# Attention and a two-layer expert on one core: short products ahead of expert pieces, 1/l ahead of the maxima, x's split spread out, and three engines' order left to the list

## Chip, cores and metric

The kernel runs on one core of a Trainium2 chip. The metric is device time in microseconds, of one launch. Lower is better.

## What is computed

For 4 batches and 8 heads of 576 positions by 64 features the reference computes causal softmax attention, mixes it with a linear memory read-out, and passes the result (2304 tokens by 512) through an expert of two matrices with a softplus between them:

```python
scores = scale * q @ k.T                      # causal mask: -1e9 above the diagonal
a = exp(scores - scores.max(-1)); a /= a.sum(-1) + 1e-09
local = a @ v
q_p = phi(q)                                  # elu(q) + 1
mem_out = (q_p @ M_prev) / (q_p @ z_prev + 1e-6)
x = g * mem_out + (1 - g) * local             # g = sigmoid(beta), one per head
h = x @ w_in                                  # 512 -> 2048
out = softplus(h) @ w_out                     # 2048 -> 512
```

## The kernel before

**Attention.** The work is cut into 16 units, one for each batch and pair of heads. A unit has four slots: the first holds query chunks 0 and 1 (128 rows each), then chunk 2, chunk 3, and the 64 rows of chunk 4. In a slot, `emit_S` puts the scores of both heads into one of two PSUM tiles `s` on TensorE (with small matmuls that add the mask), VectorE takes the row maxima (`nm`), ScalarE scales them and computes the exponentials `P` with their row sums `l`. One slot later `emit_split` forms r = 1/l on VectorE (`rr`), multiplies P by r on GpSimd into a half-precision high part, and subtracts that on VectorE into a low part (both in `PHL`). DMAs on SP's queue transpose PHL into `PTA` or `PTB`. Three slots after the chunks 0 and 1, and three after chunk 4, `emit_pv` multiplies with v into the PSUM tile `xp`, and ScalarE writes x out of it.

**Preparation of a unit.** `prep_items` spreads over the slots of the unit before: sums of |v| on ScalarE (`jk`, `sm`), a product with a matrix of means on TensorE (`sp`), five short instructions on VectorE (`sc`), phi(q) (`pe`, `ph`), v in two halves (`vb`), and the memory read-out: five products (`np`, function `f3`) whose denominators and quotient (`a`, `mem`) VectorE computes. The second part of `np` lies in the same PSUM tile as `xp`, of which there is one.

**Expert, first part.** Of the 16 blocks of 128 hidden units the first six (`GA`) are computed beside the attention for four blocks of 384 tokens. `fill_step` puts one piece into a slot: twelve matmuls for one h (`hp`), or eighteen for one output quarter (`op`). Each x block must be split first into two tiles of a reduced format (`xhl`, GpSimd casts, VectorE subtracts). `emit_g` applies softplus and splits the result into `g` on ScalarE and VectorE. The weights come as 64-bit floats; `split64` decodes them on GpSimd, VectorE and ScalarE, twelve half-blocks during the attention, let out at `WRATE` per slot.

**Expert, rest.** After the attention the remaining weights are decoded and the rest of the expert runs, with TensorE's, VectorE's, ScalarE's and GpSimd's instructions ordered by the compiler's list.

**What sets the order.** From the loads of the first unit to the end of the attention the loop in `attn_softplus_moe` writes the order by hand: TensorE, VectorE, ScalarE and GpSimd run their instructions in the order in which Python emits them (`tc.manual_schedule`), and each engine waits at the first one that isn't ready. SP's queue alone is ordered by the list: the compiler's own timing of the program decides, among the ready instructions of an engine, by the place at which they were emitted. In a slot the loop emits: the posts of the last piece (softplus and both halves of g), the scores and maxima, then `emit_split` of the slot before, the products with v that are due, the expert piece, and the preparation that is due.

Of the kernel before, what the change touches and what calls it, by code (L numbers as in the profile page):

```python
# [11 lines left out]
F32R = mybir.dt.float32r  # L12
# [17 lines left out]
GRPS = [6, 10]  # L30
NWB = 6
PVLAG = 3
WRATE = 0.6
GA = GRPS[0]


# [10 lines left out]
def attn_softplus_moe(  # L47
# [35 lines left out]
    CAP = 384  # L83
# [88 lines left out]
    def emit_g(pool, hp, n, cap, gb):  # L172
        l = pool.tile([128, cap], F32, tag="l", name="l", bufs=3)[:, :n]
        g = pool.tile([128, 2, cap], F32R, tag="g", name="g", bufs=gb)
        A.activation(out=l, in_=hp[:, :n], func=AF.Softplus)  # L175
        cast(A, g[:, 0, :n], l)
        sub(V, g[:, 1, :n], l, g[:, 0, :n])
        return g

    def out_pairs(f, g, dm, n):  # L180
        w = wt[f]
        wh, wl = w[:, 1, 0, dm * 128:(dm + 1) * 128], w[:, 1, 1, dm * 128:(dm + 1) * 128]
        return [(wh, g[:, 0, :n]), (wh, g[:, 1, :n]), (wl, g[:, 0, :n])]

    blocks, work, ready, posts = deque(), deque(), {}, deque()
    XLAG = 2

    def split_x(pool, t0, kd, xt, ea, eb):
        src = x[:, kd, t0:t0 + CAP]
# [3 lines left out]
    def push_fill(k):  # L193
        st = {}
        t0 = k * CAP

        def xs():
            st["x"] = moe1.tile([128, 2, 4, CAP], F32R, tag="xhl", name="xhl", bufs=1)
            for kd in range(4):
                split_x(moe1, t0, kd, st["x"], P, V)  # L200

        def h(f):
            hp = emit_h(moe1, f, st["x"], CAP, CAP)

            def post():
                st[f] = emit_g(moe1, hp, CAP, CAP, GA)
            return post

        def o(dm):
            op = ps_r.tile([128, 512], F32, tag="h", name="op", bufs=2)  # L210
            pairs = []
            for f in range(GA):
                pairs += out_pairs(f, st[f], dm, CAP)
            mm3(op[:, :CAP], pairs, True, True)

            def post():
                pb = moe1.tile([128, CAP], F32, tag="l", name="pb", bufs=3)
                A.copy(pb, op[:, :CAP])
                SY.dma_start(out=part[:, dm, t0:t0 + CAP], in_=pb)
            return post  # L220

        blocks.append((k, xs))
        work.extend([(12, k, h, f) for f in range(GA)] + [(3 * GA, k, o, dm) for dm in range(4)])

    def next_block(t):
        if blocks:
            k, xs = blocks.popleft()
            xs()
            done.add(k)
            ready[k] = t + XLAG  # L230

    def fill_step(t, force=False):

        if not work:
            return
        n, k, fn, j = work[0]
        if k not in done:
            next_block(t)  # L240
        if not force and ready.get(k, 1 << 30) > t:
            return
        work.popleft()
        posts.append(fn(j))
        if n == 12 and j == GA - 1:
            next_block(t)

    def run_posts():
        while posts:
            posts.popleft()()  # L250


    units = [Unit(b, p) for b in range(B) for p in range(NP)]
# [126 lines left out]
            w = 1  # L380
        return pts, l[:, :w]

    def emit_split(u, cs, pts, l):
        r = at.tile([128, 4], F32, tag="rr", name="rr", bufs=3)[:, :l.shape[1]]
        p = u.p
        if cs == (4,):
            ci = cinv4[:, p:p + 1]
        else:
            ci = cinv[:, 2 * p:2 * p + 2].unsqueeze(1).to_broadcast([128, len(cs), 2])
        V.scalar_tensor_tensor(out=r if cs == (4,) else r.rearrange("p (c h) -> p c h", h=2),  # L390
                               in0=l if cs == (4,) else l.rearrange("p (c h) -> p c h", h=2),
                               scalar=1e-9 * ESH, in1=ci, op0=ALU.add, op1=ALU.mult)
        V.reciprocal(out=r, in_=r)
        w = "A" if cs[0] < 2 else "B"
        if w not in u.pt:
            shape = [128, 8, 256] if w == "A" else [128, 18, 320]
            u.pt[w] = at.tile(shape, F16, tag="PT" + w, name="PT" + w, bufs=2 if w == "B" else 1)
        dst = u.pt[w]
        for j, c in enumerate(cs):
            pt = pts[j]  # L400
            ph = at.tile([128, (c + 1) * 512 if c < 4 else 2 * S], F16, tag=f"PHL{c}", name="PHL", bufs=1)
            if c < 4:
                nk = c + 1
                o = ph.rearrange("p (k t h s) -> p k t h s", t=2, h=2, s=128)
                for h in range(2):
                    rh = r[:, 2 * j + h:2 * j + h + 1]
                    src = pt[:, h * nk * 128:(h + 1) * nk * 128].rearrange("p (k s) -> p k s", s=128)
                    P.tensor_scalar(out=o[:, :, 0, h, :], in0=src, scalar1=rh, scalar2=0.0, op0=ALU.mult, op1=ALU.add)  # L408
                    V.scalar_tensor_tensor(out=o[:, :, 1, h, :], in0=src, scalar=rh, in1=o[:, :, 0, h, :],  # L409
                                           op0=ALU.mult, op1=ALU.subtract)  # L410
                q0 = (c - (0 if w == "A" else 2)) * 128
                SY.dma_start_transpose(out=dst[:, 0:4 * nk, q0:q0 + 128], in_=ph)
            else:
                o = ph[:, 0:1024].rearrange("p (k t s) -> p k t s", t=2, s=128)
                src = pt[:, 0:512].rearrange("p (k s) -> p k s", s=128)
                o4, s4 = ph[:, 1024:1152], pt[:, 512:576]
                P.tensor_scalar(out=o[:, :, 0, :], in0=src, scalar1=r, scalar2=0.0, op0=ALU.mult, op1=ALU.add)
                P.tensor_scalar(out=o4[:, 0:64], in0=s4, scalar1=r, scalar2=0.0, op0=ALU.mult, op1=ALU.add)
                V.scalar_tensor_tensor(out=o[:, :, 1, :], in0=src, scalar=r, in1=o[:, :, 0, :], op0=ALU.mult,
                                       op1=ALU.subtract)  # L420
                V.scalar_tensor_tensor(out=o4[:, 64:128], in0=s4, scalar=r, in1=o4[:, 0:64], op0=ALU.mult,
                                       op1=ALU.subtract)
                d = dst.rearrange("p (j h) q -> p j h q", h=2)
                for h in range(2):
                    SY.dma_start_transpose(out=d[:, :, h, 256:320], in_=ph[64 * h:64 * h + 64, 0:1152])
# [51 lines left out]
    with ExitStack():  # L477
# [3 lines left out]
        consts(bsb)  # L481
        order = ExitStack()
        order.enter_context(tc.manual_schedule(engines={
            mybir.EngineType.PE, mybir.EngineType.DVE, mybir.EngineType.Activation, mybir.EngineType.Pool}))
        loads(0)
        prep, late = {}, {}

# [18 lines left out]
        decode = deque()  # L506
        t = 0
        while t < ns or late or prev is not None:
            cur = None
            if t < ns:  # L510
                i, c = slots[t]
                u = units[i]
                if c[0] == 0 and i + 1 < len(units):
                    loads(i + 1)
                    plan(i + 1, t)
                run_posts()
                cur = (u, c) + emit_S(u, c)
                if c[0] in (0, 4):
                    late.setdefault(t + PVLAG, []).append((u, "A" if c[0] == 0 else "B"))
            else:  # L520
                run_posts()
            if prev is not None:
                emit_split(*prev)
            for a in late.pop(t, []):
                emit_pv(*a)
            fill_step(t)
            for f in prep.pop(t, []):
                f()
            if decode:
                a, b = decode.popleft()  # L530
                a()
                posts.append(b)
            wcred += WRATE
            while wcred >= 1 and pieces:
                wcred -= 1
                decode.append(pieces.popleft()())
            prev = cur
            t += 1
        run_posts()
        assert not pieces and not prep and not decode  # L540

        order.close()
        attn_ctx.close()
        while work and work[0][1] in done:
            fill_step(t, True)
            run_posts()
        wb = ctx.enter_context(tc.tile_pool(name="wb", bufs=1, side="right", reuse_waits="tile"))
        hcnt.append(0)
        moe2 = ctx.enter_context(tc.tile_pool(name="moe2", bufs=1, reuse_waits="tile"))
# [33 lines left out]
        for i in range(len(seq) + LAG):  # L583
            if i < len(seq):
                s, f = seq[i]
                fl = steps[s][2]
                fi = f - fl[0]
                hp = emit_h(moe2, f, xh[s], CAP, CAP)
                gs[i] = emit_g(moe1, hp, CAP, CAP, GA)
                for _ in range(2 if i % 3 == 0 else 1):  # L590
                    if pieces:
                        pieces.popleft()()
                if fi == 0:
                    if s == len(rest):
                        partial(s)
                    if s + 1 < len(steps):
                        partial(s + 1)
                if s + 1 < len(steps) and 1 <= fi < 5:
                    next_x(s + 1, fi - 1)
# [81 lines left out]
```

## Time and profile before

| what | value |
|---|---|
| median of 3 runs | 722.59 us (721.75 to 723.76) |
| profiled execution, its own time | 720.95 us |
| span from the first to the last instruction in the profile | 719.2 us |
| TensorE matmul busy | 599.6 us (83%) |
| VectorE busy | 413.5 us (57%) |
| ScalarE busy | 313.8 us (44%) |
| GpSimd busy | 125.9 us (18%) |
| mean granted TensorE clock | 0.898 |

The profile is one execution. PE is TensorE's matmuls, PEld its weight loads, DVE VectorE, ACT ScalarE, POOL GpSimd, SPq the DMA queue. L409 is line 409 of the kernel before. The shares are averages over two stages that differ: the attention with the expert's first part, to about 416 us, and the expert alone after it.

### The profile page before, as it was taken

The numbers are of one execution on the slowest core, as the hardware profiler recorded it, in microseconds if no ns is written. First come the engines' busy times: TensorE is split into PE (matmuls) and PEld (weight loads), VectorE is DVE, ScalarE is ACT, GpSimd is POOL, SyncE is SP. The second block draws the span as 40 slices with busy tenths as digits, with TensorE's granted clock in tenths as the row PEclk, the third lists the DMA queues.
The fourth block names the chain that finished last, engine by engine and source line by source line (L and its number), as shares of the span: only waits on it lengthen the run. The fifth ranks groups of instructions, "written<-read, shape, count | busy, mean of one in ns | idle before, by whom it ended". The sixth has DMA issues, their size and how long they took to land.

```text
span 719.2 us, 10758 instructions
## 1 busy us (share of the span) xinstructions
PE 599.6 (83%) x3928; PEld 527.3 (73%) x3928; DVE 413.5 (57%) x918; ACT 313.8 (44%) x797; POOL 125.9 (18%) x218
## 2 busy tenths in 40 slices
PE   6553553847986679989888999999999999999998
PEld 4332332636864557767666899999999999999997
DVE  4788787887578785777678368886203122220211
ACT  6444544357565564665466245444213232321221
POOL 1323223322124231223123112220000000000000
PEclk9566756769997898989999999999999999999999
DMA  5656556435576564644743455571200202010001
GB/s 186 140 123 163 149 111 164 118 72 130 119 160 129 104 128 96 152 91 100 150 85 68 101 173 192 205 226 67 73 16 23 67 0 88 1 45 1 22 23 45
DMA packets 125749, 73.87 MB, mean 103 GB/s; under 512 B 105728, under 2 KB 115456, under 8 KB 125696
## 3 DMA queue, kind: packets, MB, share of 16 engines
q1 hardware_dynamic: 125696, 73.18, 41.2%
q8 instruction: 31, 0.51, 0.3%
q14 instruction: 22, 0.18, 0.1%
HBM read 38.03 MB, written 9.44 MB: 66 GB/s over the span
## 4 chain that ended last, share of the span: by engine, by line
PE 64%; DVE 23%; ACT 5%; issue 3%; POOL 3%; DMA 1%; SPq 0%; ACTq 0%; POOLq 0%
PE hp L153 26%; PE acc L153 21%; DVE PHL L409 7%; PE op L153 7%; PE xp L443 5%; DVE nm L357 4%; DVE mem L318 2%; PE xp L433 2%; ACT P L364 2%; POOL PHL L408 2%; PE s L343 1%; DVE xhl L91 1%; PE s L370 1%; DVE wu L139 1%; DVE wu L141 1%
## 5 line engine op out<-in xcount | busy, mean ns | idle before, releaser
L153 PE MATMUL hp<-xhl,w 128*128 128x384 f32 x1152 | 220.8, 341 | 3.5 <-DVE a L315 3.5
L153 PEld LDWEIGHTS hp<-xhl,w 128*128 128x128 f32 x1152 | 202.4, 189 | 6.1 <-issue 3.7
L153 PE MATMUL acc<-g,w 128*128 128x384 f32 x864 | 161.6, 337 | 0.1
L153 PEld LDWEIGHTS acc<-g,w 128*128 128x128 f32 x864 | 151.7, 188 | 0.6 <-DVE pl L617 0.4
L91 DVE TENSOR_TENSOR g<-l,g 128x384 fp32r<-128x384 f32 x96 | 53.7, 560 | 139.9 <-ACT g L97 139.0
L175 ACT ACTIVATE l<-hp 128x384 f32<-128x384 f32 x96 | 46.9, 490 | 155.3 <-PE hp L153 153.1
L408 POOL TENSOR_SCALAR PHL<-P,rr 128x128 f16<-128x128 f32 (+3 forms) x128 | 67.9, 546 | 233.6 <-ACT nm L360 131.4
L409 DVE SCALAR_TENSOR_TENSOR PHL<-P,rr,PHL 128x128 f16<-128x128 f32 (+3 forms) x128 | 88.5, 739 | 35.4 <-POOL PHL L408 35.4
L343 PE MATMUL s<-kp,mq 64*128 64x128 f32 (+3 forms) x256 | 57.5, 536 | 27.2 <-ACT P L364 16.3
L433 PE MATMUL xp<-identf,mem 128*128 128x128 f32 (+1 forms) x80 | 21.2, 351 | 68.9 <-DVE mem L318 67.2
L433 PEld LDWEIGHTS xp<-identf,mem 128*128 128x128 f32 (+1 forms) x80 | 10.5, 167 | 80.5 <-issue 75.0
L364 ACT ACTIVATE P<-s,nm 128x128 f32<-128x128 f32 (+3 forms) x128 | 66.1, 525 | 4.1 <-ACT nm L360 0.4
L153 PE MATMUL op<-g,w 128*128 128x384 f32 x288 | 54.9, 344 | 1.0 <-DVE g L91 1.0
L357 DVE TENSOR_REDUCE nm<-s 128x2 f32<-128x256 f32 (+1 forms) x64 | 50.9, 816 | 3.7 <-PE s L352 3.7
L443 PEld LDWEIGHTS <-vb 128*64 128x64 f16 x640 | 41.5, 142 | 15.3 <-issue 3.0
L153 PEld LDWEIGHTS op<-g,w 128*128 128x128 f32 x288 | 50.0, 190 | 2.5 <-DVE g L91 1.3
L97 ACT CAST w<-wu 128x512 fp32r<-128x512 f32 x32 | 19.9, 621 | 73.3 <-DVE wu L141 73.3
L360 ACT ACTIVATE nm<-nm 128x2 f32<-128x2 f32 (+1 forms) x48 | 9.8, 204 | 96.3 <-DVE nm L357 96.3
L97 ACT CAST g<-l 128x384 fp32r<-128x384 f32 x96 | 49.2, 513 | 2.6
L343 PEld LDWEIGHTS s<-kp,mq 64*128 64x128 f32 x256 | 21.3, 203 | 37.1 <-ACT P L364 19.0
L443 PE MATMUL xp<-PTB,vb 128*64 128x320 f16 (+2 forms) x448 | 45.0, 378 | 0.0
L137 POOL TENSOR_SCALAR wu<-ws 128x512 f32<-128x512 f32 x32 | 29.3, 915 | 66.9 <-DMA ws<-in_w_in_dram 35.7
(74 smaller groups left out, 583.7 us busy)
## 6 DMA issues: line engine op xcount, KB each, us to landing
ws<-in_w_in_dram SPq DMA_DIRECT2D x16, 512.0 KB, 3.9
ws<-in_w_out_dram SPq DMA_DIRECT2D x16, 512.0 KB, 3.5
mq<-in_nat_dram SPq DMA_DIRECT2D x16, 353.0 KB, 3.4
pl<-part SPq DMA_DIRECT2D x7, 768.0 KB, 5.9
va<-in_nat_dram SPq DMA_DIRECT2D x16, 320.0 KB, 3.2
kp<-in_nat_dram SPq DMA_DIRECT2D x16, 288.0 KB, 3.7
out_dram<-pl SPq DMA_DIRECT2D x24, 192.0 KB, 1.9
part<-pb SPq DMA_DIRECT2D x16, 192.0 KB, 2.1
```

The costliest lines, as they stand in the source:

```text
L91: eng.tensor_tensor(out=out, in0=in0, in1=in1, op=ALU.subtract)
L97: A.copy(out, in_)
L137: P.tensor_scalar(out=tu, in0=sw[:, :, 1], scalar1=RB, scalar2=1.0, op0=ALU.mult, op1=ALU.mult)
L153: nc.tensor.matmul(out, lhsT=l, rhs=r, start=start and i == 0, stop=stop and i == n - 1)
L175: A.activation(out=l, in_=hp[:, :n], func=AF.Softplus)
L343: return mm(s[:, h, o:o + n], lhsT=u.qp[rows[h], c * 128:(c + 1) * 128], rhs=u.kp[rows[h], :n], start=True, stop=True, skip_group_check=True)
L357: V.tensor_reduce(out=nm[:, 2 * j:2 * j + 2], in_=s[:, :, o:o + n], op=ALU.max, axis=AX.X, negate=True)
L364: A.activation(out=pts[j][:, h * n:h * n + n], in_=s[:, h, o:o + n], func=AF.Softplus, scale=SCALE, bias=nm[:, 2 * j + h:2 * j + h + 1], a ...
L408: P.tensor_scalar(out=o[:, :, 0, h, :], in0=src, scalar1=rh, scalar2=0.0, op0=ALU.mult, op1=ALU.add)
L409: V.scalar_tensor_tensor(out=o[:, :, 1, h, :], in0=src, scalar=rh, in1=o[:, :, 0, h, :], op0=ALU.mult, op1=ALU.subtract)
L433: nc.tensor.matmul(xp[:, c * 128 - q0:min(c * 128 + 128, S) - q0], lhsT=u.mem[r, c, :], rhs=identf[r, r], start=c in (0, 2), stop=False, i ...
L443: nc.tensor.matmul(xp[r, lo:n], lhsT=u.vb[:, vi, kc, r], rhs=pt[:, kc * 4 + t * 2 + h, lo:n], start=False, stop=kc == kcs[-1] and i == len ...
```

## The change

Six edits. (1) The hand-written order is kept on TensorE alone; VectorE, ScalarE and GpSimd get the list's order too. (2) In a slot the preparation, with its short products `sp` and `np`, is emitted ahead of the expert piece. (3) The function that forms r is cut out of `emit_split` as `emit_r` and emitted ahead of the scores. (4) The low half of g is emitted after the products with v and not with the high half. (5) The four parts of an x block's split are emitted one or two to a slot, and a block that isn't fetched ahead is ready after three slots, not two. (6) `WRATE` goes from 0.6 to 0.5. What is computed stays the same, with as many instructions of each kind.

```diff
-WRATE = 0.6
+WRATE = 0.5
...
         cast(A, g[:, 0, :n], l)
-        sub(V, g[:, 1, :n], l, g[:, 0, :n])
-        return g
+        return g, lambda: sub(V, g[:, 1, :n], l, g[:, 0, :n])
...
-        def xs():
-            st["x"] = moe1.tile([128, 2, 4, CAP], F32R, tag="xhl", name="xhl", bufs=1)
-            for kd in range(4):
-                split_x(moe1, t0, kd, st["x"], P, V)
+        def xs(kd):
+            if kd == 0:
+                st["x"] = moe1.tile([128, 2, 4, CAP], F32R, tag="xhl", name="xhl", bufs=1)
+            split_x(moe1, t0, kd, st["x"], P, V)
...
             def post():
-                st[f] = emit_g(moe1, hp, CAP, CAP, GA)
+                st[f], lo = emit_g(moe1, hp, CAP, CAP, GA)
+                los.append(lo)
...
-    def next_block(t):
+    def next_block(t, step):
         if blocks:
             k, xs = blocks.popleft()
-            xs()
+            xq.extend([(t + 1 + kd // step, lambda kd=kd: xs(kd)) for kd in range(4)])
             done.add(k)
-            ready[k] = t + XLAG
+            ready[k] = t + 1 + 4 // step
...
-    def emit_split(u, cs, pts, l):
+    def emit_r(u, cs, pts, l):
         r = at.tile([128, 4], F32, tag="rr", name="rr", bufs=3)[:, :l.shape[1]]
...
         V.reciprocal(out=r, in_=r)
+        return r
+
+    def emit_split(u, cs, pts, r):
...
         order.enter_context(tc.manual_schedule(engines={
-            mybir.EngineType.PE, mybir.EngineType.DVE, mybir.EngineType.Activation, mybir.EngineType.Pool}))
+            mybir.EngineType.PE}))
...
-            cur = None
+            cur, rr = None, None
+            run(posts)
+            if prev is not None:
+                rr = emit_r(*prev)
...
             if prev is not None:
-                emit_split(*prev)
+                emit_split(*prev[:3], rr)
             for a in late.pop(t, []):
                 emit_pv(*a)
-            fill_step(t)
+            run(los)
             for f in prep.pop(t, []):
                 f()
+            fill_step(t)
+            split_due(t)
```

How instructions move is shown at three places. Numbers behind a name (`w_170`, `mask_66`) tell tiles of one kind apart. First TensorE, in a unit with expert pieces, around the memory read-out `np`. Before:

```order
L153 MATMUL hp<-xhl,w_171 128x384 x12
L314 MATMUL np<-mq,ph 128x130 x5
L343 MATMUL s<-kp,mq 128x512 x2
...
L433 MATMUL xp<-identf,mem 128x128 x2
L433 MATMUL xp<-identf,mem 128x64
...
L153 MATMUL op<-g,w_166 128x384 x3
...
L287 MATMUL sp<-sm,mean 128x1
```

With the change:

```order
L317 MATMUL np<-mq,ph 128x130 x5
L153 MATMUL hp<-xhl,w_170 128x384 x12
L346 MATMUL s<-kp,mq 128x512 x2
...
L439 MATMUL xp<-identf,mem 128x128 x2
L439 MATMUL xp<-identf,mem 128x64
...
L290 MATMUL sp<-sm,mean 128x1
...
L153 MATMUL hp<-xhl,w_171 128x384 x12
```

The expert piece of twelve now stands between `np` and the products into `xp`, and `sp` stands ahead of the next piece. Second VectorE, in the second slot of a unit, where chunk 2's maxima, the split of chunks 0 and 1 and the quotient `mem` meet. Before:

```order
L357 TENSOR_REDUCE nm<-s 128x2
L390 SCALAR_TENSOR_TENSOR rr<-l,cinv 128x4
L393 RECIPROCAL rr<-rr 128x4
L409 SCALAR_TENSOR_TENSOR PHL<-P,rr,PHL 128x128 x2
L409 SCALAR_TENSOR_TENSOR PHL<-P,rr,PHL 128x2x128 x2
L315 TENSOR_SCALAR a<-np 128x6
...
L318 TENSOR_TENSOR mem<-np,a 128x256
```

With the change:

```order
L321 TENSOR_TENSOR mem<-np,a 128x384
L321 TENSOR_TENSOR mem<-np,a 128x256
L393 SCALAR_TENSOR_TENSOR rr<-l,cinv 128x4
L308 TENSOR_TENSOR ph<-ph,pe 128x576
L396 RECIPROCAL rr<-rr 128x4
L415 SCALAR_TENSOR_TENSOR PHL<-P,rr,PHL 128x128
L360 TENSOR_REDUCE nm<-s 128x2
L415 SCALAR_TENSOR_TENSOR PHL<-P,rr,PHL 128x128
```

`mem` now stands ahead of the split, and other work stands between 1/l and the low parts. Third ScalarE, around the exponentials of chunk 4. Before:

```order
L446 ACTIVATE x<-xp,sc 128x320
L299 ACTIVATE pe<-mq 128x576
L300 ACTIVATE pe<-pe,msh 128x576
L218 COPY pb<-op 128x384
L377 ACTIVATE nm<-nm 128x1
L378 ACTIVATE P,l<-s,nm 128x576
L446 ACTIVATE x<-xp,sc 128x256
```

With the change:

```order
L452 ACTIVATE x<-xp,sc 128x320
L327 ACTIVATE vb<-va,sc 128x640
L175 ACTIVATE l<-hp 128x384
L97 CAST g<-l 128x384
L452 ACTIVATE x<-xp,sc 128x256
L380 ACTIVATE nm<-nm 128x1
L381 ACTIVATE P,l<-s,nm 128x576
```

The 256 columns of x, which wait for a product with v on TensorE, now stand ahead of chunk 4's exponentials; so it is in 15 of the 16 units, and in none before.

## Rows read from the trace of the kernel before

**Rows 1.** Stretches: start and end, length, busy us (instructions) per engine, clock, DMA, GB/s
```profile
0.00:20.00 20.00, 11.64 (x92) 8.97 (x94) 10.71 (x39) 11.19 (x31) 2.97 (x14) 0.91 0.54 178
20.00:160.00 140.00, 72.75 (x516) 46.73 (x512) 112.56 (x247) 64.10 (x175) 40.45 (x66) 0.65 0.57 132
160.00:416.00 256.00, 215.52 (x1602) 172.83 (x1604) 176.98 (x432) 142.06 (x390) 64.99 (x118) 0.91 0.55 114
416.00:719.20 303.20, 299.71 (x1727) 298.79 (x1723) 113.20 (x204) 96.49 (x201) 17.53 (x20) 1.00 0.22 74
```
**Rows 2.** Waits of VectorE, 0 to 160 us: who for whom, total us, times, longest
```profile
DVE PHL L409 <- POOL PHL L408: 11.8, 16, 0.9
DVE w L91 <- ACT w L97: 7.7, 12, 0.7
DVE sc L288 <- PE sp L287: 5.1, 3, 4.3
DVE PHL L419 <- POOL PHL L417: 4.8, 5, 1.2
```
**Rows 3.** Waits of VectorE, 160 to 416 us
```profile
DVE PHL L409 <- POOL PHL L408: 23.6, 32, 0.9
DVE sc L288 <- PE sp L287: 20.4, 7, 4.0
DVE PHL L419 <- POOL PHL L417: 9.8, 11, 0.9
```
**Rows 4.** Waits of TensorE, 0 to 160 us
```profile
PE xp L433 <- DVE mem L318: 34.8, 5, 8.3
PE s L343 <- ACT P L378: 10.5, 5, 4.6
```
**Rows 5.** Waits of TensorE, 160 to 416 us
```profile
PE xp L433 <- DVE mem L318: 32.5, 9, 6.6
```
**Rows 6.** Timeline of TensorE, two units: start, us, instruction, count, idle before it
```profile
296.61 0.61 PE L433 MATMUL xp<-identf,mem 128*128 128x128 f32 x3 [0.69 <-DVE mem L318]
297.15 1.72 PE L443 MATMUL xp<-PTB,vb 128*64 128x320 f16 x28
298.80 2.39 PE L153 MATMUL hp<-xhl,w 128*128 128x384 f32 x12
...
318.18 0.96 PE L433 MATMUL xp<-identf,mem 128*128 128x128 f32 x3 [3.57 <-DVE mem L318]
319.06 3.20 PE L443 MATMUL xp<-PTB,vb 128*64 128x320 f16 x28
322.20 3.28 PE L153 MATMUL hp<-xhl,w 128*128 128x384 f32 x12
```
**Rows 7.** Stretches of these two units, columns as in Rows 1
```profile
296.60:301.00 4.40, 4.39 (x43) 3.79 (x43) 2.69 (x5) 3.25 (x8) 1.15 (x2) 1.00 0.22 63
...
318.10:322.20 4.10, 4.02 (x32) 2.79 (x32) 3.23 (x6) 1.65 (x5) 1.15 (x2) 0.50 0.22 41
```
**Rows 8.** Groups of VectorE by form: busy us, mean ns of one, idle before
```profile
L409 DVE SCALAR_TENSOR_TENSOR PHL<-P,rr,PHL 128x512 f16<-128x512 f32 x32 | 30.8, 1001 | 14.2 <-POOL PHL L408 14.2
L139 DVE SCALAR_TENSOR_TENSOR wu<-ws,wu 128x512 int32<-128x512 int32 x32 | 22.5, 704 | 0.8
```
**Rows 9.** Timeline of VectorE: one form, beside GpSimd (first) and alone (second)
```profile
90.19 0.66 DVE L421 SCALAR_TENSOR_TENSOR PHL<-P,rr,PHL 128x64 f16<-128x64 f32 x1
...
310.65 0.27 DVE L421 SCALAR_TENSOR_TENSOR PHL<-P,rr,PHL 128x64 f16<-128x64 f32 x1
```
**Rows 10.** Timeline: products behind chunk 4's scores, an output piece, ScalarE's x
```profile
280.48 0.44 PE L433 MATMUL xp<-identf,mem 128*128 128x128 f32 x2
280.84 0.69 PE L443 MATMUL xp<-PTA,vb 128*64 128x256 f16 x12
281.46 3.40 PE L153 MATMUL op<-g,w 128*128 128x384 f32 x18
...
403.61 0.46 ACT L446 ACTIVATE x<-xp,sc 128x256 f32<-128x256 f32 x1
```

More of the change, by code (lines that the diff above doesn't have):

```diff
@@ L183, in out_pairs @@
         return [(wh, g[:, 0, :n]), (wh, g[:, 1, :n]), (wl, g[:, 0, :n])]
-    blocks, work, ready, posts = deque(), deque(), {}, deque()
-    XLAG = 2
+    blocks, work, ready, posts, los, xq = deque(), deque(), {}, deque(), deque(), deque()
     def split_x(pool, t0, kd, xt, ea, eb):
@@ L239, in fill_step @@
         if k not in done:
-            next_block(t)
+            next_block(t, 2)
         if not force and ready.get(k, 1 << 30) > t:
@@ L245, in fill_step, with split_due, run @@
         if n == 12 and j == GA - 1:
[L246 to L250, printed above, removed]
+            next_block(t, 1)
+    def split_due(t):
+        while xq and xq[0][0] <= t:
+            xq.popleft()[1]()
+    def run(q):
+        while q:
+            q.popleft()()
     units = [Unit(b, p) for b in range(B) for p in range(NP)]
@@ L515, in attn_softplus_moe @@
                     plan(i + 1, t)
-                run_posts()
                 cur = (u, c) + emit_S(u, c)
@@ L519, in attn_softplus_moe @@
                     late.setdefault(t + PVLAG, []).append((u, "A" if c[0] == 0 else "B"))
-            else:
-                run_posts()
             if prev is not None:
-                emit_split(*prev)
+                emit_split(*prev[:3], rr)
             for a in late.pop(t, []):
                 emit_pv(*a)
-            fill_step(t)
+            run(los)
             for f in prep.pop(t, []):
                 f()
+            fill_step(t)
+            split_due(t)
             if decode:
@@ L538, in attn_softplus_moe @@
             t += 1
-        run_posts()
+        run(posts)
+        run(los)
+        split_due(t + 9)
         assert not pieces and not prep and not decode
@@ L545, in attn_softplus_moe @@
             fill_step(t, True)
-            run_posts()
+            run(posts)
+            run(los)
+            split_due(t + 9)
         wb = ctx.enter_context(tc.tile_pool(name="wb", bufs=1, side="right", reuse_waits="tile"))
@@ L588, in attn_softplus_moe @@
                 hp = emit_h(moe2, f, xh[s], CAP, CAP)
-                gs[i] = emit_g(moe1, hp, CAP, CAP, GA)
+                gs[i], lo = emit_g(moe1, hp, CAP, CAP, GA)
+                lo()
                 for _ in range(2 if i % 3 == 0 else 1):
```

## The prediction

> **What bounds the kernel now.** I read the stretches first. From 416 us on, TensorE is busy for 299.71 of 303.20 us at full clock [rows 1]: the expert's rest runs against TensorE, the change leaves its work alone, and I take this stage as fixed. What can move ends at 416 us. There no engine is full. From 20 to 160 us, where almost no expert piece runs, VectorE is busy for 112.56 of 140 us and TensorE for 72.75 at a mean clock of 0.65. From 160 to 416 us, with the expert pieces, TensorE is busy for 215.52 of 256 us at 0.91, and VectorE for 176.98 [rows 1].
>
> Second, the waits, to see why neither is full. VectorE stands at the head of its hand-written order: for GpSimd's high part in every slot, for ScalarE's cast of a weight, for TensorE's `sp` [rows 2, 3]. TensorE stands for VectorE's `mem` (34.8 us in five times early, 32.5 in nine later) and, early, for exponentials [rows 4, 5]. This is a ring. The products with v need the one tile `xp`, which VectorE frees only when `mem` is computed from `np`; before, `np` comes behind an expert piece, and only one slot's scores lie between it and `xp`. Then VectorE needs `sp`, which stands behind the products with v and one more piece. Each makes the other late. So I read the first stretch as VectorE's, where its waits are time, and the second as the ring's, where TensorE's waits are time.
>
> Third, the clock. After a wait of 3.57 us for `mem`, TensorE's next 4.10 us were granted 0.50, which is the lower of its two levels (1.2 GHz), and the transposes, the 28 products and the expert piece took 0.96, 3.20 and 3.28 us; one unit earlier, after a wait of 0.69 us, they were granted 1.00 (2.4 GHz) and took 0.61, 1.72 and 2.39 [rows 6, 7]. A long wait thus cost 0.35 + 1.48 + 0.89 = 2.7 us behind itself.
>
> **The change, part by part.** Nothing is removed or added; every term is a wait that shrinks or one that is made.
>
> A. VectorE's list order and 1/l ahead of the maxima, first stretch. The waits that other ready work can fill are 11.8 + 7.7 + 5.1 + 4.8 = 29.4 us [rows 2]. With the change `ph` and a maximum stand between 1/l and the low parts, so GpSimd's multiplication goes on behind useful work. Bounds: 0, if each wait only moves to the next instruction, and 29.4, if all are filled. A fixed order made by the compiler's timing will not fit the chip everywhere, so I take the middle: -14.7 us. If these go, what is late next is TensorE with scores (`s` has two tiles); at 72.75 busy in 140 us it has room.
>
> B. Short products ahead of the piece, second stretch. The piece of twelve, 2.39 us, or of eighteen, 3.40 [rows 6, 10], now stands between `np` and `xp`, and covers that much of VectorE's way to `mem`. Nine waits of 3.6 us in the mean (32.5 / 9) lose about 2.35 each: -21 us. Bounds: 0, if VectorE reaches `a` later by as much, and -40.5, all of TensorE's idle time there (256 - 215.52). What VectorE waits for `sp`, 20.4 us [rows 3], is the other half of the same ring and isn't counted again.
>
> C. The clock behind those waits. Nine waits at 2.7 us are 24 us; the mean clock says the same: 256 x (1 - 0.91) = 23 us. The waits get shorter and don't vanish, so I take a third: -8 us; bounds 0 and -24.
>
> D. GpSimd and VectorE at once. Before, VectorE mostly stood still while GpSimd worked on the first half (35.4 us in 409's two rows, 14.6 in 419's [rows 2, 3]). With the change it works, and that isn't free: a low part of 64 columns took 0.66 us beside GpSimd's decoding and 0.27 alone [rows 9], and the low parts of 512 columns, which run beside GpSimd's second half, take 1001 ns in the mean where a two-input instruction of 512 columns of the decoding takes 704 [rows 8]. At one new collision per unit it is 16 x 0.39 = +6 us; bounds 0 and, at four per unit, +25. The Trainium skill, page "SBUF — State Buffer", section "Who interferes with whom", says that a VectorE instruction with two SBUF inputs and a GpSimd instruction that reads SBUF can't run together, and that the second to issue is blocked fully until the first is done. By it this term would be near its upper bound and the sum -14.7 - 21 - 8 + 25 = -19 us. The two rows agree in direction, and the rule speaks against the change (second rival).
>
> E. The rest. The low half of g behind the products with v, the split spread over slots, and the decoding at 0.5 per slot move places in a list that runs ahead by itself: cover is VectorE's idle time of 79 us in the second stretch (256 - 176.98). Blocks 0 and 1 start a slot later, so one more piece lies behind the last scores, where pieces already stand between products: 0, at most one piece of eighteen, +3.4 us [rows 10]. SP's queue was the list's before and holds the same transfers; its DMA share of 0.57 and 0.55 [rows 1] rises with the shorter stage to some 0.62, which is not full. ScalarE's order puts x ahead of chunk 4's exponentials: 0 here, and the third rival if not.
>
> **The sum.** -14.7 - 21 - 8 + 6 = -37.7 us. The profiled execution took 720.95 us, so 683.2; the median of the runs is 722.59, 1.6 above it, so I forecast **685 us**. Its own range is 668 to 702: the three gains, 43.7 us together, smaller or larger by 40%.
>
> **The rivals.**
>
> First, *VectorE becomes nearly full and the ring opens altogether.* For it: VectorE's busy time to 416 us is 10.71 + 112.56 + 176.98 = 300 us, TensorE's 300 at a clock well below full [rows 1], so both have room for a stage of 350 us. Against it: a fixed order. With the whole of A and three quarters of B's and C's bounds (30 and 18) it is -29.4 - 30 - 18 + 6 = -71; with two thirds of that -48. So 651 to 675, say 662.
>
> Second, *the shared way to SBUF takes back what the waits give.* If every wait on GpSimd returns as a longer VectorE instruction, A keeps only half of 7.7 + 5.1, which is 6.4, and D goes to +25 from 6; -6.4 - 21 - 8 + 25 = -10, or 712 us for the runs. For it are rows 8 and 9, and the skill's rule; against it, that maxima and `mem`, read from PSUM, are much of VectorE's work and can stand there, and that the low parts already pay for this today.
>
> Third, **slower**: *ScalarE stands at the head of its new order.* In 15 units the x of chunks 0 and 1, which needs TensorE's 0.44 + 0.69 us of products behind chunk 4's scores [rows 10], stands ahead of chunk 4's exponentials, and these free the score tile that TensorE takes two slots later, and give VectorE its sums. With x's own 0.46 us that is some 1.6 us later per unit. TensorE waits for these exponentials today, 10.5 us in five units [rows 4]. If it is exposed everywhere, and drops the clock each time, it costs 15 x (1.6 + 2.7) = 64 us, against a gain of 37.7: +27, so 749 us. It decides from 37.7 / 15 = 2.5 us per unit on. Against it: those products follow the scores directly, so part of the 1.13 us passes while VectorE still forms chunk 4's maximum.
>
> Fourth, *it doesn't do what it says.* The list could give back nearly the old order, or fill one wait by making the next: 722 us. The order of the change shows that rows do move, so this is small.
>
> **How the numbers follow.** Forecast 0.43, first rival 0.17, second 0.20, third 0.16, fourth 0.04. The forecast, the first and the second rival are faster by more than 0.3% (2.2 us, about what a measurement of this kernel can tell from no change): 0.80, of which I move 0.02 to slower, since the unknown order can fail in places I haven't listed: 0.78, 0.04, 0.18. The range leaves out the slower cases and the lower third of the first rival: 660 to 724.
>
> **What would show it.** In the profile after, the stretch with TensorE full must begin near 378 us and still last about 303. VectorE's waits for GpSimd, 50 us in all, should be under 25, and its wait for `sp` under 10; TensorE's waits for `mem`, 67 us in all, under 40; the clock in the filled units above 0.91. Right for the second rival would be low parts well over 1001 ns, and other two-input groups longer by a tenth or more, with VectorE's busy sum up by 20 us. The third rival would show as ScalarE waiting for `xp` in chunk 4's slot, and TensorE's wait for L381 above 10.5 us. I am wrong in the reading itself if the waits go and the attention still ends near 416 us, or if the last stage gets longer than 303 us.

## The result, and the profile after

| what | before | with the change |
|---|---|---|
| median of 4 runs, us | 722.17 (721.39 to 723.76) | 676.65 (672.16 to 683.31) |
| ratio | 1 | 0.9346 [0.9294, 0.9398] |
| profiled execution / span, us | 720.95 / 719.2 | 677.64 / 675.9 |
| TensorE matmul busy, us | 599.6 (83%) | 592.9 (88%) |
| VectorE / GpSimd busy, us | 413.5 / 125.9 | 389.4 / 139.3 |
| mean granted clock | 0.898 | 0.932 |

The change saves 45.5 us by the medians and 6.5% by the ratio; the forecast's sum was 37.7 us. (The slowest of the four runs was in a slower state and isn't in the ratio.) To see where the time went, both spans have to be cut at equal work and not at equal times: at the first scores of unit 5 (units count from 0), where the expert pieces begin to fill the slots, and at the run of 38 `hp` matmuls that follows the attention's last products. Stretches of the kernel before, cut there; columns as in [rows 1]:

```profile
20.00:134.50 114.50, 58.43 (x418) 36.35 (x414) 90.88 (x200) 53.12 (x145) 33.37 (x55) 0.63 0.59 139
134.50:416.90 282.40, 230.74 (x1719) 184.01 (x1715) 198.66 (x479) 153.05 (x421) 72.07 (x130) 0.90 0.54 113
416.90:719.20 302.30, 298.81 (x1710) 298.00 (x1708) 113.20 (x204) 96.49 (x201) 17.53 (x20) 1.00 0.22 75
```

The same stretches of the changed kernel:

```profile
20.00:122.40 102.40, 56.71 (x431) 34.22 (x427) 88.39 (x217) 52.96 (x149) 41.98 (x61) 0.71 0.65 150
122.40:370.70 248.30, 224.10 (x1711) 178.72 (x1708) 176.57 (x464) 146.93 (x417) 78.50 (x125) 0.94 0.63 131
370.70:675.90 305.20, 300.99 (x1717) 299.97 (x1715) 112.45 (x200) 95.02 (x197) 15.30 (x20) 1.00 0.22 72
```

The early stretch is 12.1 us shorter and the filled one 34.1, of which 27.5 are TensorE's idle time (51.66 to 24.20) and 6.6 its busy time, with eight matmuls fewer and a clock of 0.94 for 0.90. The last stretch is 2.9 longer: 2.2 of that is busy time, of which seven more matmuls on this side of the cut, at some 0.18 us each, explain 1.3; its idle time grew by 0.7. Together that is 43.3 us, the difference of the two spans.

Waits of VectorE in the changed kernel, to the end of the attention (they answer to [rows 2, 3]):

```profile
DVE rr L393 <- ACT P L367: 23.7, 16, 4.1
DVE sc L291 <- PE sp L290: 12.4, 9, 2.9
DVE PHL L415 <- POOL PHL L414: 9.9, 16, 0.9
...
DVE PHL L425 <- POOL PHL L423: 8.0, 9, 0.9
DVE rr L393 <- ACT P L381: 7.5, 6, 2.6
```

The waits for GpSimd fell from 50.0 to 17.9 us, the one for `sp` from 25.5 to 12.4. A new one, of which before has 0.4 us, is 31.2 us in two rows: VectorE for ScalarE's exponentials, in front of 1/l. Waits of TensorE, first to 122.4 us, then to the attention's end (they answer to [rows 4, 5]):

```profile
PE xp L439 <- DVE mem L321: 14.4, 2, 7.2
PE s L346 <- ACT P L367: 11.8, 3, 4.3
...
PE s L346 <- ACT P L381: 4.9, 4, 2.1
```
```profile
PE xp L439 <- DVE mem L321: 12.8, 7, 3.4
PE s L346 <- ACT P L367: 4.0, 2, 2.0
...
PE s L346 <- ACT P L381: 1.2, 3, 0.9
```

By these rows `mem` cost 67.3 us before and 27.2 now. One wait more belongs to it: the trace puts 2.1 us in front of `xp` in the last unit to `rr` (L396), which VectorE ran just behind `mem` and ended 0.08 us after it. With that one it is 29.3, and 14.9 in the filled stretch. The wait for L381, one of the third rival's signs, is 6.1.

### The profile page after: what moved, and what is told of

Same layout as the page of the kernel before. It is cut to its first block, busy times and chain, and to the rows that moved or that the text cites. A ratio compares the mean times of both kernels' runs of the same rounds, so it can differ in the third digit from the quotient of the medians.

```text
span 675.9 us, 10788 instructions
## 1 busy us (share of the span) xinstructions
PE 592.9 (88%) x3928; PEld 522.1 (77%) x3928; DVE 389.4 (58%) x918; ACT 308.6 (46%) x797; POOL 139.3 (21%) x218
## 4 chain that ended last, share of the span: by engine, by line
PE 40%; DVE 7%; DMA 3%; issue 2%; ACT 2%; POOL 1%; SPq 0%; POOLq 0%; DVEq 0%; ACTq 0%
PE acc L153 19%; PE hp L153 17%; DMA ws<-in_w_in_dram 2%; PE op L153 2%; PE xp L449 1%; DVE wu L139 1%; DVE wu L141 1%; DVE PHL L415 1%; DMA ws<-in_w_out_dram 1%; ACT P L367 1%; DVE g L91 1%; POOL wu L137 1%; DVE nm L360 1%; DVE xhl L91 1%; DVE wu L138 1%
## 5 line engine op out<-in xcount | busy, mean ns | idle before, releaser
L414 POOL TENSOR_SCALAR PHL<-P,rr 128x128 f16<-128x128 f32 (+3 forms) x128 | 86.2, 688 | 143.0 <-ACT x L452 24.8
L346 PE MATMUL s<-kp,mq 64*128 64x128 f32 (+3 forms) x256 | 59.2, 550 | 32.5 <-ACT P L367 15.8
L415 DVE SCALAR_TENSOR_TENSOR PHL<-P,rr,PHL 128x128 f16<-128x128 f32 (+3 forms) x128 | 79.5, 641 | 10.1 <-POOL PHL L414 9.9
L449 PEld LDWEIGHTS <-vb 128*64 128x64 f16 x640 | 40.1, 133 | 21.2 <-DMA PTA<-PHL 6.9
L346 PEld LDWEIGHTS s<-kp,mq 64*128 64x128 f32 x256 | 22.0, 210 | 43.3 <-ACT P L367 28.8
L439 PE MATMUL xp<-identf,mem 128*128 128x128 f32 (+1 forms) x80 | 20.0, 333 | 33.2 <-DVE mem L321 27.2
L137 POOL TENSOR_SCALAR wu<-ws 128x512 f32<-128x512 f32 x32 | 23.8, 743 | 107.4 <-DMA ws<-in_w_in_dram 56.0
L449 PE MATMUL xp<-PTB,vb 128*64 128x320 f16 (+2 forms) x448 | 41.4, 352 | 2.6 <-DMA PTB<-PHL 2.6
L91 DVE TENSOR_TENSOR xhl<-x,xhl 128x384 fp32r<-128x384 f32 x48 | 25.6, 578 | 25.3 <-ACT xhl L97 23.4
```

What stands on the lines that cost most here:

```text
L91: eng.tensor_tensor(out=out, in0=in0, in1=in1, op=ALU.subtract)
L137: P.tensor_scalar(out=tu, in0=sw[:, :, 1], scalar1=RB, scalar2=1.0, op0=ALU.mult, op1=ALU.mult)
L346: return mm(s[:, h, o:o + n], lhsT=u.qp[rows[h], c * 128:(c + 1) * 128], rhs=u.kp[rows[h], :n], start=True, stop=True, skip_group_check=True)
L439: nc.tensor.matmul(xp[:, c * 128 - q0:min(c * 128 + 128, S) - q0], lhsT=u.mem[r, c, :], rhs=identf[r, r], start=c in (0, 2), stop=False, i ...
L449: nc.tensor.matmul(xp[r, lo:n], lhsT=u.vb[:, vi, kc, r], rhs=pt[:, kc * 4 + t * 2 + h, lo:n], start=False, stop=kc == kcs[-1] and i == len ...
```

## Experiments

The theory is the prediction's: the list fills VectorE's early waits, the products ahead of the piece shorten the ring in the filled stretch, and the two add. Against it stand that the list does it alone; that the emitted order does it and the list is not needed; that a third edit carries it; and that the shared way to SBUF sets the price. Each kernel differs from before or from the change by the few lines shown. The kernel before was timed again beside them, so kernels are best compared by their ratios to it; a difference of medians can be off from that by up to 4 us. "Unit 5" and "end" are the two cuts, in us of the profiled execution.

| kernel | unit 5 | end | median, us | ratio to before |
|---|---|---|---|---|
| before | 134.5 | 416.9 | 722.17 | 1 |
| the change | 122.4 | 370.7 | 676.65 | 0.9346 [0.9294, 0.9398] |
| e1: before, list on three engines | 121.9 | 406.3 | 713.27 | 0.9890 [0.9856, 0.9925] |
| e2: change, four engines by hand | 119.5 | 373.1 | 681.51 | 0.9450 [0.9418, 0.9481] |
| e3: change, piece first again | 122.8 | 398.5 | 709.61 | 0.9851 [0.9812, 0.9891] |
| e4: change, 1/l late again | 122.9 | 371.5 | 677.10 | 0.9389 [0.9355, 0.9423] |
| e5: before, products ahead | 133.3 | 412.1 | 716.61 | 0.9930 [0.9903, 0.9956] |
| e6: before, `np` out of `xp`'s tile | 133.1 | 393.6 | 698.24 | 0.9675 [0.9656, 0.9693] |
| e7: change, `np` out of `xp`'s tile | 117.0 | 355.8 | 663.65 | 0.9194 [0.9167, 0.9220] |
| e8: change, GpSimd's high parts twice | 136.4 | 399.4 | 705.98 | 0.9776 [0.9743, 0.9808] |
| e9: before, 1/l ahead | 120.0 | 384.2 | 694.17 | 0.9624 [0.9603, 0.9646] |
| e10: before, both ahead | 121.1 | 381.5 | 689.48 | 0.9557 [0.9541, 0.9574] |
| e11: e7, x's casts on ScalarE | 114.9 | 356.6 | 661.74 | 0.9178 [0.9155, 0.9202] |
| e12: e2, `np` out of `xp`'s tile | 112.6 | 349.7 | 658.56 | 0.9141 [0.9126, 0.9156] |

**e1, the list alone.**

```diff
-            mybir.EngineType.PE, mybir.EngineType.DVE, mybir.EngineType.Activation, mybir.EngineType.Pool}))
+            mybir.EngineType.PE}))
```

> The kernel before, with VectorE, ScalarE and GpSimd left to the list and nothing else. Theory 1 (two causes that add: the list fills VectorE's waits, the short products ahead open the ring): some 20 us less than before, about 702 us, with VectorE's waits for GpSimd (50 us before) under 25, but TensorE's waits for mem between 160 us and the end of the attention still above 25 us. Theory 2 (the list alone does it): about 677 us, as the whole change. Theory 3 (the order of emission alone): 722 us.

Unit 5 begins at 121.9, as in the change, but the filled stretch takes 284.4 us where before took 282.4. Waits of its TensorE and VectorE, 20 to 400 us:

```profile
PE xp L433 <- DVE mem L318: 53.5, 10, 9.1
...
DVE rr L390 <- ACT P L364: 36.2, 25, 3.8
DVE sc L288 <- PE sp L287: 20.6, 10, 4.6
DVE PHL L409 <- POOL PHL L408: 14.4, 22, 0.9
```

The list fills VectorE's waits for GpSimd (14.4 and 6.8 us are left of 50), makes new ones in front of 1/l, and in the filled stretch leaves `mem` as it was (39.3 us, before 37.9). The early gain can be had from the list alone; of the filled stretch's gain it gives nothing.

**e2, the order by hand.** The same line the other way round, in the changed kernel.

> The whole change, but with the order of all four engines kept as written by hand. Theory 1: some 25 us less than before, about 697 us, since the piece covers mem and 1/l goes ahead, while VectorE still stands at the head of its order for the cast of a weight and for TensorE. Theory 2: 722 us or more. Theory 3: about 677 us.

It is 5 us slower than the change by the medians and 7.5 by the ratios: nearly the whole gain comes without the list.

**e3, the piece ahead of the products again.**

```diff
-            for f in prep.pop(t, []):
-                f()
             fill_step(t)
+            for f in prep.pop(t, []):
+                f()
             split_due(t)
```

> The whole change, but the expert piece again ahead of the preparation in a slot, so that np and sp stand behind it on TensorE. Theory 1: 15 to 20 us more than the change, about 694 us, with TensorE's waits for mem in the filled units back from 13 to over 25 us. Theory 2: within 4 us of the change, 677 us. Theory 3: nearly all is lost, above 710 us.

33 us are lost by the medians; of the 27.7 us between the two profiled executions 27.4 lie in the filled stretch. All three runs missed theory 1's times (702, 697 and 694 us were expected). In the list's order the place of the products is worth nearly everything there: without it the other edits are worth so little beside the list that the intervals of e1 and e3 overlap.

**e4, 1/l back at the head of the split.**

```diff
-            if prev is not None:
-                rr = emit_r(*prev)
...
-                emit_split(*prev[:3], rr)
+                emit_split(*prev[:3], emit_r(*prev))
```

> The whole change, but 1/l emitted behind the maxima again, at the head of the split. If the place of 1/l in the list counts (theory 1 with edit 3): 4 to 8 us more than the change, and VectorE's waits for GpSimd up from 18 to 30 us. If the list moves it by itself (theory 2): within 4 us of the change.

No difference is shown (the intervals overlap), not even in VectorE's waits for GpSimd (9.9 and 8.0 us, as in the change). The list doesn't need the place at which 1/l is emitted.

**e5, products ahead of the piece, alone and by hand.**

```diff
-            fill_step(t)
             for f in prep.pop(t, []):
                 f()
+            fill_step(t)
```

> The kernel before with one edit: the preparation, with np and sp, emitted ahead of the expert piece in a slot; all four engines in hand order. Theory 1 now (the ring through the tile xp sets the filled units, the place of 1/l sets the early ones): the filled units gain as in the change, 25 to 30 us, the early ones nothing, so about 694 us, with unit 5 starting at 135 us as before. Rival (the ring opens only if VectorE is early too, through 1/l or the list): under 12 us gained, above 710 us.

This was the theory's worst miss: 5.5 us where the filled stretch's whole gain was expected. The wait for `mem` stays at 63.3 us:

```profile
PE xp L433 <- DVE mem L318: 63.3, 14, 8.3
```

The timelines tell why e3 and e5 disagree. TensorE's timeline at the read-out of unit 9 in each kernel: start and us first, the time waited in brackets. Before:

```profile
236.66 1.28 PE L314 MATMUL np<-mq,ph 128*128 128x130 f32 x10
237.86 1.13 PE L343 MATMUL s<-kp,mq 64*128 64x512 f32 x4
...
244.99 0.96 PE L433 MATMUL xp<-identf,mem 128*128 128x128 f32 x3 [5.89 <-DVE mem L318]
```

The same in e5, where a piece runs behind `np`:

```profile
232.64 1.38 PE L314 MATMUL np<-mq,ph 128*128 128x130 f32 x10
233.78 2.33 PE L153 MATMUL hp<-xhl,w 128*128 128x384 f32 x12
...
242.61 0.96 PE L433 MATMUL xp<-identf,mem 128*128 128x128 f32 x3 [5.33 <-DVE mem L318]
```

The piece now runs inside, and `xp` waits nearly as long: 9.97 us lie between the two starts where 8.33 lay. With VectorE's order fixed by hand, `a` and `mem` keep their place behind the split of chunks 0 and 1, and an earlier `np` buys little. Now e3, where the list orders VectorE and the piece still comes first:

```profile
214.06 1.28 PE L317 MATMUL np<-mq,ph 128*128 128x130 f32 x10
...
219.44 0.61 PE L439 MATMUL xp<-identf,mem 128*128 128x128 f32 x3 [2.85 <-DVE mem L321]
```

And the change:

```profile
205.30 1.38 PE L317 MATMUL np<-mq,ph 128*128 128x130 f32 x10
206.44 2.33 PE L153 MATMUL hp<-xhl,w 128*128 128x384 f32 x12
...
210.17 0.61 PE L439 MATMUL xp<-identf,mem 128*128 128x128 f32 x3
```

5.38 us without the piece, 4.87 with it inside, and a wait of 0.07 us is left. Means over units 6 to 14, the nine later waits of the prediction, worked out from the timelines (the second column counts all of TensorE's idle time in front of `xp`, also where the trace names `rr`, as it mostly does in e2, e9 and e10):

| kernel | `np` to `xp`, us | of it TensorE waits |
|---|---|---|
| before | 6.25 | 3.61 |
| e5: products ahead, by hand | 8.10 | 3.04 |
| e3: list, piece first | 6.74 | 3.43 |
| the change: list, products ahead | 6.47 | 1.43 |
| e9: 1/l ahead, by hand | 5.03 | 2.27 |
| e10: both ahead, by hand | 7.06 | 2.11 |
| e2: all edits, by hand | 6.93 | 1.53 |

In the list's order the way from `np` to `xp` is as long with the piece inside it as without, so the piece takes the place of 2.0 of the 3.4 us of waiting. By hand the way grows by most of what is put into it (6.25 to 8.10, 5.03 to 7.06). The products ahead need an engine behind them that takes `mem` earlier. It need not be the list that does it: with all edits the order by hand waits hardly longer in these units than the change (e2, 1.53 us).

**e6 and e7, the ring by itself.** The second part of `np` gets a tile of the two of `hp` and `op` and no longer the one of `xp`; nothing else moves.

```diff
-            t = ps_r.tile([128, 3, 130], F32, tag="xp" if c0 else "sm", name="np", bufs=1)[:, 0:k]
+            t = ps_r.tile([128, 3, 130], F32, tag="h" if c0 else "sm", name="np", bufs=2 if c0 else 1)[:, 0:k]
```

> The kernel before with one edit: the second part of np lies in one of the two tiles of the expert's h and no longer in the tile of the products with v; order unchanged. Theory 1 (the wait for mem is for the tile, not for its values): TensorE's waits for mem, 67 us, all but vanish, and 20 to 30 us are gained, about 696 us. Rival (TensorE is late because VectorE is, and waits then at the next tile, the scores): the wait moves to the scores and under 8 us are gained, above 714 us.

> The change with the same edit. Theory 1: the 27 us of waits for mem that the change left go, with 10 to 20 us of time, about 662 us. Rival: the wait moves to the scores, 677 us within 4 us.

On before it saves 24 us, on the change 13 by the medians (11 by the ratios). Waits of TensorE in e6, 20 to 400 us, the three longest:

```profile
PE xp L433 <- ACT x L446: 26.0, 13, 6.0
PE s L343 <- ACT P L378: 10.3, 5, 3.3
PE s L343 <- ACT P L364: 9.7, 5, 4.8
```

The wait for `mem` is gone. So the ring ran through the shared tile, as the prediction read it. The early stretch stayed as it was (unit 5 at 133.1 for 134.5), although 29.4 us of waits for `mem` went there too: in it those waits were not time, as the prediction had said, and nearly all of the gain is in the filled stretch, 260.5 us for 282.4. What is late next is ScalarE's x, which frees `xp`.

**e8, GpSimd's work doubled.** Each high part of chunks 0 to 3 is computed a second time, into a tile that nothing reads: 128 more GpSimd instructions.

```diff
+                    ex = at.tile([128, 4, 128], F16, tag="ex", name="ex", bufs=1)[:, 0:nk]
+                    P.tensor_scalar(out=ex, in0=src, scalar1=rh, scalar2=0.0, op0=ALU.mult, op1=ALU.add)
```

> The change with each of the 128 high parts on GpSimd computed a second time into a tile that nobody reads: some 70 to 85 us more of GpSimd work, for which it has room (139 us busy in 676). Second rival of the prediction (GpSimd and VectorE stand in each other's way): VectorE's low parts and its other two-input instructions get longer by a tenth or more, its busy sum rises by 15 us or more, and the time by 10 to 25 us. Without such a cost: within 4 us of the change.

GpSimd's busy time goes from 139.3 to 233.0 us, 33% of the span, and the kernel is 29 us slower than the change, more than the 10 to 25 that were expected. VectorE's longest form of low parts, first in the change, then in e8:

```profile
L415 DVE SCALAR_TENSOR_TENSOR PHL<-P,rr,PHL 128x512 f16<-128x512 f32 x32 | 29.1, 925 | 4.6 <-POOL PHL L414 4.6
```
```profile
L417 DVE SCALAR_TENSOR_TENSOR PHL<-P,rr,PHL 128x512 f16<-128x512 f32 x32 | 34.1, 1068 | 10.8 <-POOL PHL L414 10.7
```

These low parts get longer by 15%, VectorE's busy time rises by 20.5 us and its waits for GpSimd's high parts by 11.0 (17.9 to 28.9): the second rival's signs. That the two sums together are near the loss doesn't show that they are the loss. How much of it comes from the two engines slowing each other, and how much from the second head's high part standing behind the extra instruction, this run doesn't separate.

**e9 and e10, 1/l ahead by hand, alone and with the products.**

```diff
+            if prev is not None:
+                rr = emit_r(*prev)
...
-                emit_split(*prev)
+                emit_split(*prev[:3], rr)
```

> The kernel before with one edit: 1/l emitted ahead of the scores and maxima, so GpSimd's high parts run under the next maximum; hand order on four engines. If this edit is what saves the early units in hand order: unit 5 starts near 120 us where it started at 135, the waits of VectorE for GpSimd fall from 50 us to under 15, and the time is about 705 us. Rival (the place of 1/l does nothing, as it does nothing in the list): above 716 us.

> The kernel before with two edits, 1/l ahead of the scores and the preparation ahead of the piece; hand order. If the two only add: the saving of 1/l alone plus 5 us. If VectorE must be early for the covered mem to help (the two enable each other): 15 us or more beyond that sum, about 685 us, near the hand order with all edits (681.5 us).

Of the three edits tried alone (e1, e5, e9) e9 gives the largest gain, 3.8% [3.5, 4.0], more than was expected (694 us for 705): unit 5 at 120.0, and the filled stretch 18.2 us shorter. Wait of VectorE for GpSimd in e9, 20 to 384 us:

```profile
DVE PHL L412 <- POOL PHL L411: 1.0, 4, 0.3
```

Before, this wait took 35.4 us; and with less of VectorE's time ahead of `mem`, the way from `np` to `xp` falls to 5.03 us. The products ahead add 4.7 us to it, about what they gave alone (5.5): by hand the two don't help each other. From e10 to e2, another 8 us by the medians, are the later low half of g, the spread split, the lower `WRATE`, and the last piece's posts, which e2 emits ahead of 1/l and e10 behind it; they weren't tried apart.

**e11 and e12, versions that beat the change.** e11 puts the casts of x's split on ScalarE in e7; e12 is e6's line in e2.

```diff
-            split_x(moe1, t0, kd, st["x"], P, V)
+            split_x(moe1, t0, kd, st["x"], A, V)
```

> The change with the second part of np in a tile of h, and the casts of the x split on ScalarE in place of GpSimd (16 of some 690 ns). If GpSimd's work costs VectorE's: 94 us more of it cost 29 us, so 11 us less give some 3 to 4 us back, about 660 us against 663.7. If ScalarE is what is late instead: 664 us or more.

> The change in hand order on four engines with the second part of np in a tile of h. If the list counts for little once the tile is apart: within 6 us of 663.7 us. If the list's gain (4.9 us in the change) comes from what the ring hides: 675 us or more.

e11's interval overlaps e7's, so its 2 us are not shown. e12 is the fastest of all, 658.56 us, 2.2% under the change by the ratios, and 5 us under e7, which has the list (4 by the ratios). Its stretches:

```profile
112.60:349.70 237.10, 220.19 (x1708) 176.82 (x1707) 190.77 (x484) 154.10 (x426) 74.88 (x133) 0.95 0.66 138
349.70:658.50 308.80, 302.83 (x1717) 301.50 (x1716) 112.00 (x200) 95.23 (x197) 16.22 (x20) 0.99 0.21 71
```

TensorE stands idle for 16.9 us of the filled stretch (237.10 - 220.19) where the change had 24.2 and before 51.7. With the tile apart, the order by hand is better than the list by 4 to 5 us; without it, worse by 5 to 7. Its last stretch, 308.8, is longer than the 302.3 of before, 4.0 us of it busy time (with seven more matmuls) and 2.5 idle; why is open.

## Why the prediction was right, and where it wasn't

The sign, the range and the forecast's own range held; 685 was forecast and 676.65 measured. Step by step:

**What bounds the kernel.** Right. TensorE fills from 370.7 where 378 was forecast, and e6 shows the ring by opening it. The last stage nearly stayed: at 305.2 us it is over the 303 that the prediction set as a sign of a wrong reading. Of the 2.9 us more than before at the same cut, 1.3 are the seven matmuls that moved behind it; the rest is open.

**Term A, the list and 1/l ahead, -14.7: measured -12.1, but the two are one lever and not two.** Either alone brings unit 5 to nearly the same place: the list 121.9 (e1), 1/l ahead by hand 120.0 (e9), both 122.4. The list keeps its gain without the place of 1/l (e4). The step "if all are filled" also left out a price: in the list's order VectorE waits 31.2 us for exponentials in front of 1/l, before 0.4. And the term was for the first stretch alone, where 1/l ahead by hand takes 18.2 us from the filled one too (e9), since `mem` comes earlier; the sum had nothing for that.

**Term B, products ahead of the piece, -21: the wait for `mem` in the filled stretch fell by 23.0 us (37.9 to 14.9, at equal work).** The size was right and the condition missing, that VectorE is free to take `a` and `mem` earlier. The bound "0, if VectorE reaches `a` later by as much" is nearly what happens in the order by hand (e5: 8.10 us for 6.25), and "covers that much of VectorE's way" what happens in the list's (the change against e3: 33 us). The prediction put the list into A and the products into B, and summed them as if each worked alone: alone they give 8.6 (e1) and 5.5 us (e5), together far less than the 45.5 of the change. That the term came out is in part luck: the change happens to carry the condition that the sum didn't name.

**Term C, the clock, -8: measured -6.6** as TensorE's busy time in the filled stretch (about 1 us of it is the eight matmuls fewer), at 0.94 where "above 0.91" was asked. The size was right, the way not quite: in units 6 to 14 the 28 products behind `mem` took 2.7 to 3.2 us and not 1.72 in seven of nine before, and in seven of nine with the change, though the waits are shorter (1.43 us for 3.61 in the mean). What fell is the time at the lower level. As an estimate from the mean clocks, with levels of 1.00 and 0.50, it went from 56 us of 282 (0.10 / 0.50) to 30 of 248 (0.06 / 0.50).

**Term D, GpSimd and VectorE at once, +6: on the wrong engine.** The low parts were to get longer; they got shorter, and GpSimd's high parts longer. GpSimd's longest form, before and with the change:

```profile
L408 POOL TENSOR_SCALAR PHL<-P,rr 128x512 f16<-128x512 f32 x32 | 21.9, 696 | 84.1 <-ACT nm L377 76.1 <-DVE rr L393 5.4 <-issue 2.7
```
```profile
L414 POOL TENSOR_SCALAR PHL<-P,rr 128x512 f16<-128x512 f32 x32 | 28.6, 905 | 45.3 <-ACT x L452 24.8 <-ACT P L367 12.2 <-ACT vb L327 3.6
```

GpSimd pays 209 ns here in the mean and VectorE's low parts went from 1001 ns [rows 8] to 925, while `vb` on VectorE went from 873 to 997. VectorE's busy time fell by 24 us instead of rising by 6. Of these, 11.0 are the low parts, which took 107.8 us in sum and take 96.8. The times of all its instructions, added up, fell by 11.4 only (450.1 to 438.7); the rest is neighbours that overlap more in the record.

The means hide two kinds of instructions. One pair of before, a high part and the low part that starts 0.06 us behind it, and then a low part with GpSimd idle:

```profile
282.46 0.70 POOL L408 TENSOR_SCALAR PHL<-P,rr 128x512 f16<-128x512 f32 x1
282.52 1.17 DVE L409 SCALAR_TENSOR_TENSOR PHL<-P,rr,PHL 128x512 f16<-128x512 f32 x1 [0.89 <-POOL PHL L408]
283.61 0.74 DVE L409 SCALAR_TENSOR_TENSOR PHL<-P,rr,PHL 128x512 f16<-128x512 f32 x1
```

And in the change the other way round, VectorE's `vb` first and GpSimd's high part behind it; the last row is a high part with no two-input instruction beside it:

```profile
202.42 0.86 DVE L330 SCALAR_TENSOR_TENSOR vb<-va,sc,vb 128x640 f16<-128x640 f32 x1
202.65 1.19 POOL L414 TENSOR_SCALAR PHL<-P,rr 128x512 f16<-128x512 f32 x1 [2.03 <-ACT nm L380]
356.88 0.69 POOL L423 TENSOR_SCALAR PHL<-P,rr 128x512 f16<-128x512 f32 x1 [4.63 <-issue]
```

The first of a pair keeps its time, and the second ends 0.53 and 0.56 us after the first. The Trainium skill, page "SBUF — State Buffer", section "Who interferes with whom", has the second of the two wait until the first is done; here the trace agrees. So the price per collision was real, and the step that failed is "one new collision per unit": before had them already. Of the 48 low parts of 512 columns 20 took 0.98 us or more before, each ending 0.53 to 0.55 us after a GpSimd instruction, and 15 do with the change. Of GpSimd's 48 high parts of that size none was delayed before and 14 are now, and GpSimd has the room. So the second rival's price wasn't asked; in e8, where GpSimd has more to do, 26 of the 48 low parts are delayed.

**Term E, the rest, 0:** not separated by runs on the change, and the list with the products ahead wasn't tried without these edits. By hand they are worth some 8 us together (e10 to e2).

**The rivals.** The first, the ring opening altogether, is what e7 and e12 do (663.65 and 658.56; 662 was its time), by another way than it named: a tile of its own and not the order. Of the third's two signs one came: ScalarE waits for `xp` in chunk 4's slot in eight units, 8.6 us in all, where before it did in none. TensorE didn't feel it: 6.1 us of waits for L381 where over 10.5 was the mark. Of the forecast's marks two failed: the wait for `sp` is 12.4 us, not under 10, and the last stage is over 303 us.

## What to carry to other kernels

An engine that waits for a value may be waiting for the tile: look which tiles the late value shares, and give it one apart, before moving work; here that was worth 24 us alone, 13 on top of the change, and 23 on top of the change's order by hand. Work put ahead to cover a wait covers it only if the engine that answers is free to answer earlier; in a fixed order the answer must be moved too. The list and a better order by hand can be substitutes: time each alone before their gains are added.

## What the hardware showed that was not expected

The wait in front of an instruction doesn't tell by itself what clock it gets. TensorE's timeline of the changed kernel, three filled units:

```profile
178.55 0.96 PE L439 MATMUL xp<-identf,mem 128*128 128x128 f32 x3 [2.01 <-DVE mem L321]
179.43 2.90 PE L449 MATMUL xp<-PTB,vb 128*64 128x320 f16 x28
...
195.73 0.96 PE L439 MATMUL xp<-identf,mem 128*128 128x128 f32 x3 [0.27 <-DVE mem L321]
196.61 3.00 PE L449 MATMUL xp<-PTB,vb 128*64 128x320 f16 x28
...
347.06 0.61 PE L439 MATMUL xp<-identf,mem 128*128 128x128 f32 x3 [2.12 <-DVE rr L396]
347.60 1.72 PE L449 MATMUL xp<-PTB,vb 128*64 128x320 f16 x28
```

The 28 products take 2.90 us after a wait of 2.01 and 3.00 after one of 0.27, but after one of 2.12 the 1.72 of full clock [rows 6]. In front of the second TensorE was at full clock for 5.70 us and busy for 3.42 of them, as the stretch shows:

```profile
190.00:195.70 5.70, 3.42 (x26) 2.04 (x27) 4.11 (x16) 5.14 (x18) 1.96 (x5) 0.99 0.94 195
195.70:199.70 4.00, 3.97 (x35) 2.97 (x35) 3.62 (x8) 0.98 (x4) 1.38 (x3) 0.59 0.33 55
```

There it had waited 2.03 us for exponentials. Term C took a wait for `mem` by itself, and for gone with it the fall of the clock; here another wait stands in front of the same fall. Which of them lowers the clock, no run here shows.

And GpSimd, busy for only a third of the span in e8, goes with a loss of 29 us. In the pairs under term D its high parts take turns with VectorE's low parts and `vb`, and whichever starts second pays; so a new order can move the price from one engine to the other without an instruction changed.
